# Turning the third and fourth chunks of a layer norm through DRAM and VectorE

## The chip, the cores and the metric

The kernel runs on one core of one Trainium2 chip. The metric is the time of one execution in microseconds (us) of device time. Engines carry the names of the profile: PE (TensorE, matmuls; PEld its weight loads), DVE (VectorE), ACT (ScalarE), POOL (GpSimd) and SP (SyncE, which issues every transfer of this kernel).

## The reference

One transformer block on `x` of 2048 tokens by 512 values: a linear attention and a gated product, each behind a layer norm that six vectors modulate, computed from a condition `c`.

```python
def _A_ref(x, wqkv, wo):                      # 32 heads of 16
    q, k, v = ...                             # x @ wqkv
    phi = lambda t: jnp.where(t > 0, t + 1, jnp.exp(t)) + 1e-6
    pq, pk = phi(q), phi(k)
    kv = jnp.einsum("bhsd,bhse->bhde", pk, v)
    z = jnp.einsum("bhsd->bhd", pk)
    o = jnp.einsum("bhqd,bhde->bhqe", pq, kv) / (jnp.einsum("bhqd,bhd->bhq", pq, z)[..., None] + 1e-6)
    return ... @ wo

def _B_ref(x, w_gate, w_up, w_down):
    return ((x @ w_gate) * (x @ w_up)) @ w_down

sa, ca, ga, sb, cb, gb = ...                  # silu(c) @ w_mod
h = _layernorm(x) * (1 + ca) + sa
x = x + ga * _A_ref(h, A_wqkv, A_wo)
h = _layernorm(x) * (1 + cb) + sb
x = x + gb * _B_ref(h, B_w_gate, B_w_up, B_w_down)
```

## The kernel before

The 2048 tokens are four chunks of four tiles; a tile is 128 tokens by 512 values, tile `i` belongs to chunk `i // 4`. Every fp32 operand of a matmul is split into a high and a low part (`split`: ScalarE copies the high part, VectorE subtracts for the low one), and a product is three matmuls: high by high, high by low, low by high. A projection (`proj`) is 12 matmuls into one PSUM bank.

The order on each engine is the order in which the code is written out; no scheduler moves anything. An engine works through its own queue in that order and waits at an instruction whose operands are not there. SP's queue of transfers is such a queue too.

The changed code is the loop over `i` from 0 to 15 (lines 525 to 587), which makes the keys. In turn `i` it projects the keys of tile `i + 2` (`ahead`), makes their feature map (`k_phi`: two ScalarE passes, `phi_a`, and one VectorE pass, `phi_b`), splits the normalized tile and the keys of tile `i + 1` (`k_split_x` gives `xh` and `xl`, `k_split` gives `kh` and `kl`), adds the keys into `z` (`z_add`) and multiplies the keys of tile `i` with its normalized values (`t_tile`, 12 matmuls into the four accumulators `tacc`). The table `q_at` puts projections of query tiles in between, `extra` the splits of the weights `wv` and `wo` and the sums of the other modulation vectors (`mod_part`).

A projection needs the normalized chunk turned, so that the 512 values lie on the partitions. `Norm` does it in steps: `stats` (VectorE), `rstd_of` (VectorE, then a power on GpSimd), `nmr_of` (VectorE), `xhat` (ScalarE, one pass for each tile), `transpose` (TensorE, four transposes of 128 by 128 into one bank for each of four blocks `k`) and `modulated` (ScalarE scales and shifts the bank into `f`, VectorE casts the high part and subtracts the low one). For chunk 1, 2 and 3 the transposes stand in the loop, eight in each of two turns (`turn_at`): turns 1 and 2 for chunk 1, 4 and 5 for chunk 2, 8 and 9 for chunk 3. The first projection that needs chunk 2 is that of key tile 8, in turn 6; for chunk 3 it is key tile 12, in turn 10.

Behind the loop the row sum of `z` (`row_sum`, split just before) gives `zb`; from it and the accumulators come four tiles `n`, which are split and multiplied with `wv` (`kvps`, 128 by 128 matmuls). The rest of the kernel (from line 636) uses `wo`, turns queries (partly through DRAM: `move_out`, `move_in`, `turn_v`), and runs the second layer norm and the gated product. There, for the last two chunks, the way that the change uses is in place already: tiles go to DRAM, come back with their 32 by 32 blocks moved, VectorE turns each block in place into `wide` (`flip`), and ScalarE takes a row of blocks out of it, scaled and shifted (`flipped`).

Tiles of SBUF come from one pool of 94 buffers (`B`), banks of PSUM from two pools of four.

Of the kernel before, what the change touches and what calls it, by code (L numbers as in the profile page):

```python
# [24 lines left out]
def tile_adaln_block(  # L25
# [42 lines left out]
    def f32(ap):  # L68
        return ap.bitcast(F32)
# [7 lines left out]
    def B(tag, shape=(P, D), dt=F32):  # L77

        return T(tiles, tag, shape, dt)
# [4 lines left out]
    def bank():  # L84
        return T(ps_w, "bank")
# [20 lines left out]
    wide = consts.tile([P, NJ, D], F32, name="wide")  # L106
# [86 lines left out]
    def split(src, h, l, low=None):  # L193
        nc.scalar.activation(h, src, AF.Copy)  # L194
        (low or nc.vector).tensor_tensor(l, src, f32(h), op=ALU.subtract)  # L195
# [23 lines left out]
    def by_row(x):  # L219
        return x.rearrange("p (q s i) -> p s q i", q=NQ, i=BL)  # L220
# [96 lines left out]
                self.t[k] = (h, l)  # L317


    NT = NCH * NJ  # L320
    norm = [Norm(xts[0])]
    wk, wq, wv = [], [], []
    kx, phk, phq, q_ps = {}, {}, {}, {}

    def proj(i, w, of=bank):

        ch, j = divmod(i, NJ)
        ps = of()
# [14 lines left out]
    def k_split_x(i):  # L343
        ch, j = divmod(i, NJ)
        kx[i] = [B("xh", dt=F32R), B("xl", dt=F32R)]
        split(norm[ch].n[j], *kx[i])

    def k_phi(i, ps):
        phi = B("phi")
# [11 lines left out]
    def k_split(i):  # L361
        h, l = B("kh", dt=F32R), B("kl", dt=F32R)
        phi = phk[i]
        nc.scalar.activation(h, phi, AF.Identity, bias=eps_phi)
# [17 lines left out]
    def q_b(i):  # L382
        phi_b(q_ps.pop(i), phq[i])
# [28 lines left out]
    ca = col_out(1, ps_ca, 1.0)  # L412
# [3 lines left out]
    sa = consts.tile([P, KD], F32, name="col0")  # L416
# [47 lines left out]
    nx = Norm(xts[1])  # L464
# [36 lines left out]
    def mod_load(*vs):  # L501
        raw_m.update({v: load_mod(v) for v in vs})

    def mod_part(v, *ks):
        if 0 in ks:
            accs[v] = B("f")
        mod_acc(accs[v], raw_m[v], ks)
# [9 lines left out]
             12: lambda: (mod_part(4, 2, 3), wo_s.extend(split_raw(x) for x in raw_o[:2]), cols.update({3: col_out(3, mod_col(accs[3], bank()), 0.0)}), mod_load(5)),  # L517
             13: lambda: (mod_part(5, 0, 1, 2), wo_s.extend(split_raw(x) for x in raw_o[2:]), cols.update({4: col_out(4, mod_col(accs[4], bank()), 1.0)})),
             14: lambda: (mod_part(5, 3),)}
    pairs = {}  # L520
    q_at = {3: 0, 4: 1, 6: 2, 7: 3}
    ahead = {2: k_ps[2], 3: k_ps[3]}
    turn_at = {4 * ch + j: (ch + 1, 2 * j, 2 * j + 1) for ch in range(1, NCH - 1) for j in range(2)}
    turn_at.update({1: (1, 0, 1), 2: (1, 2, 3)})
    for i in range(NT):
        ch, j = divmod(i, NJ)
        done = 0
        if i > 2:
            ahead[i + 2] = proj(i + 2, wk) if i + 2 < NT else proj(i + 6 - NT, wq)
        if i in q_at:  # L530
# [7 lines left out]
        fresh = i > 0 and ch + 1 < NCH and j == 0  # L538
        if i == 2:
            turn_x()  # L540
            wq.extend(split_blocks(r) for r in raw_q)
        if fresh:
            nx.xhat(2)
        if 0 < i < NT - 1:
            k_split_x(i + 1)
        if fresh:
            nx.xhat(3)
        if 0 < i < NT - 1:
            k_split(i + 1)
        if i in turn_at and i != 2:  # L550
            t_tile(i, 0, 1)
            done = 2
            turn_x()
        if i == 2:
            t_tile(i, *range(KD))
            done = KD
            ahead[i + 2] = proj(i + 2, wk)
        if ch + 2 < NCH and j == 2:
            nx2 = Norm(xts[ch + 2])
            nx2.stats(0, 1)  # L560
        if ch + 2 < NCH and j == 3:
            nx = nx2
            nx.stats(2, 3)
            nx.rstd_of()
            nx.nmr_of()
            nx.xhat(0, 1)
        if i + 2 < NT:
            k_phi(i + 2, ahead.pop(i + 2))
        else:
            q_a(i + 6 - NT, ahead.pop(i + 2))  # L570
            q_b(i + 6 - NT)
        if i in q_at:
            q_a(q_at[i], qps)
            q_b(q_at[i])
        if i + 1 < NT:
            z_add(i + 1)
        if i == NT - 2:
            pairs["z"] = split_raw(zacc, low=nc.gpsimd)
        if i == NT - 1:
            zps = row_sum(pairs["z"])  # L580
            zb = consts.tile([P, D], F32, name="zb")
            nc.scalar.activation(zb, zps, AF.Identity, bias=eps_z)
            zq = B("z")
            nc.gpsimd.tensor_copy(zq.rearrange("p (q s i) -> p q s i", q=NQ, i=BL), by_block(zb))
        t_tile(i, *range(done, KD))
        if i in extra:
            extra[i]()
    ga, sb, cb = rows[2], cols[3], cols[4]
# [130 lines left out]
    def move_out(*tiles):  # L719

        for i in tiles:
            moved[i] = tc.dram_tile([P, D], F32, name=f"moved_{i}")
            nc.sync.dma_start(moved[i], phq.pop(i))

    def move_in(*tiles):

        for i in tiles:
            v = moved[i].rearrange("(m i) (q c) -> q i m c", i=BL, c=P)
            moved[i] = B("u")
            for q in range(NQ):  # L730
                nc.sync.dma_start(moved[i][q * BL:(q + 1) * BL].rearrange("i (m c) -> i m c", c=P), v[q])

    def turn_v(i):

# [163 lines left out]

    def flip(ch, *js):
        for j in js:  # L900
            nc.vector.transpose(wide[:, j].rearrange("p (m s i) -> p m s i", m=NQ, i=BL),
                                blocks.pop((ch, j)).rearrange("p (m s i) -> p m s i", m=NQ, i=BL))

    def flipped(ch, *ks):
        for k in ks:
            f = B("f")
            nc.scalar.activation(f.rearrange("p (x i) -> p x i", i=BL),
                                 wide.rearrange("p j (m s i) -> p (j m) s i", m=NQ, i=BL)[:, :, k],
                                 AF.Identity, scale=cb[:, k:k + 1], bias=sb[:, k:k + 1])
            blocks[ch, "f", k] = f  # L910

    stowed, blocks = {}, {}

# [403 lines left out]
    first[0].sum("s1", "s3", on=nc.gpsimd)  # L1317
    g(lambda: turn_v(13))
    y_seed(13, y_bank)
    norm2[2].xhat_blocks(2, 3)  # L1320
    turn_h(13)
    turn_l(13)
    move_in(14, 15)
    stow(2, 0, 1, 2, 3)
# [107 lines left out]
```

## Time and profile before

| | |
|---|---|
| time, median of 3 runs | 554.86 us (554.34 to 554.95) |
| the profiled execution's own time | 554.37 us |
| its span, from the first to the last instruction | 552.7 us |
| PE busy | 547.0 us (99%), 2488 matmuls |
| DVE, ACT, POOL busy | 373.6 us (68%), 291.7 us (53%), 203.4 us (37%) |
| transfers | 58.28 MB, mean 105 GB/s |
| granted TensorE clock | 1.000 |

A row of a group reads: line, engine, operation, result `<-` operands, count, then busy time and the mean time of one in ns. A row of the timeline reads: start and length in us, engine, line, operation, and in brackets how long the engine had waited and for whom. A row of one line's instructions gives the shortest, the median and the longest in ns. A row of windows gives, for a stretch of time, the sum of busy time, then each engine's busy time and instructions, the granted clock, and the transfer engines' share and rate. The matmuls overlap, so a matmul's length is longer than what it adds to the queue. Names are those of the program, with buffer numbers left out.

### The profile page before, as it was taken

How to read it: one execution, taken by the hardware profiler on the slowest of the kernel's cores; microseconds unless marked ns; L12 is line 12 of the kernel's file. 1: busy time of each engine (PE TensorE's matmuls, PEld its weight loads, DVE VectorE, ACT ScalarE, POOL GpSimd, SP SyncE). 2: the span in 40 equal slices, each digit the busy share in tenths (PEclk: the TensorE clock that was granted, in tenths of full speed). 3: DMA queues.
4: the chain of work that ended last, by engine and by line, in shares of the span. 5: the costliest groups of instructions: out<-in, count | busy, mean ns of one | idle time of the engine just before them, and what ended most of it. 6: DMA issues, size and time to landing. Idle time of an engine off the chain costs nothing.

```text
span 552.7 us, 7324 instructions
## 1 busy us (share of the span) xinstructions
PE 547.0 (99%) x2488; PEld 449.2 (81%) x2488; DVE 373.6 (68%) x610; ACT 291.7 (53%) x539; POOL 203.4 (37%) x204
## 2 busy tenths in 40 slices
PE   8999999999999999999999999999999999999997
PEld 7788888888888878878888888877888888888886
DVE  7896968986887886778776576985444444434434
ACT  3695856646476667566684545454443444444110
POOL 2000000102003201057596666766666546446200
PEclk9999999999999999999999999999999999999999
DMA  8900203320503205845545071690434222200004
GB/s 284 387 15 2 76 20 103 108 77 1 157 2 133 96 5 186 267 145 135 160 111 155 0 230 38 216 322 2 133 116 132 59 57 59 58 20 0 1 0 152
DMA packets 58373, 58.28 MB, mean 105 GB/s; under 512 B 7328, under 2 KB 38304, under 8 KB 58336
## 3 DMA queue, kind: packets, MB, share of 16 engines
q1 hardware_dynamic: 58336, 57.83, 33.2%
q8 instruction: 19, 0.31, 0.2%
q14 instruction: 18, 0.15, 0.1%
HBM read 42.60 MB, written 15.20 MB: 105 GB/s over the span
## 4 chain that ended last, share of the span: by engine, by line
PE 99%; DVE 0%; issue 0%
PE bank L1030 33%; PE acc L766 7%; PE acc L1110 6%; PE acc L1111 6%; PE acc L1112 6%; PE bank L207 5%; PE bank L209 5%; PE bank L208 5%; PE acc L375 3%; PE acc L374 3%; PE acc L373 3%; PE bank L849 2%; PE bank L851 2%; PE bank L850 2%; PE acc L146 2%; PE bank L293 2%
## 5 line engine op out<-in xcount | busy, mean ns | idle before, releaser
L1030 PE MATMUL bank<-h,w 128*128 128x512 f32 (+1 forms) x798 | 184.7, 390 | 0.0
L1030 PEld LDWEIGHTS bank<-h,w 128*128 128x128 f32 (+1 forms) x798 | 148.4, 186 | 33.4 <-ACT bank L1035 0.7
L1035 ACT ACTIVATE bank<-bank 128x512 f32<-128x512 f32 (+1 forms) x38 | 22.2, 583 | 139.6 <-PE bank L1030 139.5
L836 DVE TENSOR_TENSOR x<-acc,x 128x512 f32<-128x512 f32 (+1 forms) x73 | 48.8, 682 | 48.4 <-PE acc L1112 47.7
L1016 POOL TENSOR_TENSOR w<-raw,w 128x256 fp32r<-128x256 f32 (+3 forms) x38 | 40.9, 1077 | 91.0 <-ACT w L1009 91.0
L1111 PE MATMUL acc<-w,kh 128*128 128x512 f32 (+2 forms) x154 | 59.6, 387 | 0.0
L1110 PE MATMUL acc<-w,kh 128*128 128x512 f32 (+2 forms) x154 | 59.6, 387 | 0.0
L1112 PE MATMUL acc<-w,kl 128*128 128x512 f32 (+2 forms) x154 | 59.5, 386 | 0.0
L263 POOL TENSOR_TENSOR rstd<-ve,half 128x4 f32<-128x4 f32 (+1 forms) x10 | 11.0, 1103 | 121.8 <-DVE ve L262 69.6
L195 POOL TENSOR_TENSOR w<-raw,w 128x512 fp32r<-128x512 f32 (+1 forms) x25 | 35.1, 1409 | 52.2 <-ACT w L194 47.3
L1016 POOL TENSOR_TENSOR w<-t,w 128x512 fp32r<-128x512 f32 (+1 forms) x38 | 49.2, 1318 | 0.0
L195 DVE TENSOR_TENSOR kl<-u,kh 128x512 fp32r<-128x512 f32 (+1 forms) x38 | 26.4, 736 | 30.6 <-ACT kh L194 30.6
L207 PE MATMUL bank<-w,h 128*128 128x512 f32 x104 | 40.9, 394 | 0.0
L209 PE MATMUL bank<-w,h 128*128 128x512 f32 x104 | 40.6, 391 | 0.0
L208 PE MATMUL bank<-w,h 128*128 128x512 f32 x104 | 40.6, 390 | 0.0
L766 PE MATMUL acc<-w,xh 128*128 128x512 f32 x120 | 37.4, 393 | 0.0
L1089 DVE TENSOR_TENSOR u<-bank,u 128x512 f32<-128x512 f32 (+1 forms) x19 | 13.1, 691 | 31.6 <-PE bank L1030 25.1
L1110 PEld LDWEIGHTS acc<-w,kh 128*128 128x128 f32 (+1 forms) x154 | 28.9, 188 | 6.0
L1112 PEld LDWEIGHTS acc<-w,kl 128*128 128x128 f32 (+1 forms) x154 | 28.9, 188 | 5.9
L1111 PEld LDWEIGHTS acc<-w,kh 128*128 128x128 f32 (+1 forms) x154 | 28.9, 188 | 5.9
L998 POOL TENSOR_TENSOR t<-raw,t 128x256 f32<-128x256 f32 (+1 forms) x34 | 25.9, 761 | 1.4
L766 PEld LDWEIGHTS acc<-w,xh 128*128 128x128 f32 x120 | 22.2, 188 | 4.6
(211 smaller groups left out, 1116.5 us busy)
## 6 DMA issues: line engine op xcount, KB each, us to landing
raw<-in_w_mod_dram SPq DMA_DIRECT2D x24, 256.0 KB, 3.7
raw<-in_B_w_down_dram SPq DMA_DIRECT2D x20, 256.0 KB, 3.2
raw<-in_B_w_gate_dram SPq DMA_DIRECT2D x36, 128.0 KB, 3.4
raw<-in_B_w_up_dram SPq DMA_DIRECT2D x36, 128.0 KB, 3.4
x<-in_A_x_dram SPq DMA_DIRECT2D x16, 256.0 KB, 5.4
out_dram<-x SPq DMA_DIRECT2D x15, 256.0 KB, 2.6
raw<-in_A_wqkv_dram SPq DMA_DIRECT2D x12, 256.0 KB, 5.4
moved<-h SPq DMA_DIRECT2D x12, 256.0 KB, 2.1
```

Source lines behind the costliest of these rows:

```text
L195: (low or nc.vector).tensor_tensor(l, src, f32(h), op=ALU.subtract)
L207: nc.tensor.matmul(ps, ah, bh, start=i == 0, stop=False)
L208: nc.tensor.matmul(ps, ah, bl, start=False, stop=False)
L209: nc.tensor.matmul(ps, al, bh, start=False, stop=i == n - 1)
L766: nc.tensor.matmul(yps[i], x, y, start=False, stop=k == KD - 1 and x is al, skip_group_check=True)
L836: nc.vector.tensor_tensor(xt[:, a:b], dn[j][:, a:b], xt[:, a:b], op=ALU.add)
L998: sub = lambda out, x, y: (on or nc.gpsimd).tensor_tensor(out, x, y, op=ALU.subtract)
L1016: sub = lambda out, x, y: (on or nc.gpsimd).tensor_tensor(out, x, f32(y), op=ALU.subtract)
L1030: mm = lambda x, y, **kw: nc.tensor.matmul(ps, x[:, k], y, skip_group_check=True, **kw)
L1110: nc.tensor.matmul(ps, hh[:, a:b], dh[:n, c:d], start=i == 0, stop=False)
L1111: nc.tensor.matmul(ps, hh[:, a:b], dl[:n, c:d], start=False, stop=False)
L1112: nc.tensor.matmul(ps, hl[:, a:b], dh[:n, c:d], start=False, stop=i == len(hs) - 1)
```

## The change

Chunks 2 and 3 (`LIFTED`) are no longer transposed by TensorE. Their normalized tiles are written blockwise by ScalarE (`xhat_blocks`), go to DRAM (`lift_out`), come back in four reads each (`lift_in`), are turned by VectorE into `wide` (`lift_turn`), and four rows are taken out by ScalarE (`lift_row`) and split (`lift_parts`: the high part on ScalarE for even rows, on VectorE for odd ones). `k_split_x` reads these chunks' tiles in the blocks' order. Chunk 2's statistics are taken for two tiles at a time, in turns 2 and 3; chunk 3's all in turn 6. The rows of chunk 2 are made in turn 5, those of chunk 3 in turn 9. In turns 6 and 10 the query projection stands in front of the key projection; query tile 4 is projected in turn 10, not in turn 14. The splits of `wo` move from turns 12 and 13 to turns 14 and 15. Some helpers that stood twice in the code are now shared, and one ScalarE pass late in the kernel (`turn_h(13)`) comes in front of two others.

```diff
+    LIFTED = (2, 3)
+    def lift_out(name, x):
+        to = tc.dram_tile([P, D], F32, name=name)
+        nc.sync.dma_start(to, x)
+        return to
+    def lift_in(of):
+        v = of.rearrange("(m i) (q c) -> q i m c", i=BL, c=P)
+        u = B("u")
+        for q in range(NQ):
+            nc.sync.dma_start(u[q * BL:(q + 1) * BL].rearrange("i (m c) -> i m c", c=P), v[q])
+        return u
+    def lift_turn(j, u):
+        nc.vector.transpose(wide[:, j].rearrange("p (m s i) -> p m s i", m=NQ, i=BL),
+                            u.rearrange("p (m s i) -> p m s i", m=NQ, i=BL))
+    def lift_row(k, scale, shift):
+        f = B("f")
+        nc.scalar.activation(f.rearrange("p (x i) -> p x i", i=BL),
+                             wide.rearrange("p j (m s i) -> p (j m) s i", m=NQ, i=BL)[:, :, k],
+                             AF.Identity, scale=scale[:, k:k + 1], bias=shift[:, k:k + 1])
+        return f
+    def lift_parts(k, f, cast=True):
+        h, l = B("h", dt=F32R), B("h", dt=F32R)
+        if k % 2 and cast:
+            nc.vector.tensor_copy(h, f)
+        else:
+            nc.scalar.activation(h, f, AF.Copy)
+        nc.vector.tensor_tensor(l, f, f32(h), op=ALU.subtract)
+        return h, l
...
-        split(norm[ch].n[j], *kx[i])
+        if ch not in LIFTED:
+            split(norm[ch].n[j], *kx[i])
+            return
+        x = by_row(norm[ch].n[j])
+        h, l = (t.rearrange("p (s q i) -> p s q i", q=NQ, i=BL) for t in kx[i])
+        nc.scalar.activation(h, x, AF.Copy)
+        nc.vector.tensor_tensor(l, x, f32(h), op=ALU.subtract)
...
-             12: lambda: (mod_part(4, 2, 3), wo_s.extend(split_raw(x) for x in raw_o[:2]), ...
-             13: lambda: (mod_part(5, 0, 1, 2), wo_s.extend(split_raw(x) for x in raw_o[2:]), ...
-             14: lambda: (mod_part(5, 3),)}
+             12: lambda: (mod_part(4, 2, 3), ...
+             13: lambda: (mod_part(5, 0, 1, 2), ...
+             14: lambda: (mod_part(5, 3), wo_s.extend(split_raw(x) for x in raw_o[:2])),
+             15: lambda: wo_s.extend(split_raw(x) for x in raw_o[2:])}
-    q_at = {3: 0, 4: 1, 6: 2, 7: 3}
+    q_at = {3: 0, 4: 1, 6: 2, 7: 3, 10: 4}
-    turn_at = {4 * ch + j: (ch + 1, 2 * j, 2 * j + 1) for ch in range(1, NCH - 1) for j in range(2)}
-    turn_at.update({1: (1, 0, 1), 2: (1, 2, 3)})
+    turn_at = {1: (1, 0, 1), 2: (1, 2, 3)}
     for i in range(NT):
         ch, j = divmod(i, NJ)
-        if i > 2:
+        up = ch + 1 if 0 < ch < NCH - 1 else None
+        if i in (6, 10):
+            qps = proj(q_at[i], wq)
+        if i > 2 and i != NT - 2:
             ahead[i + 2] = proj(i + 2, wk) if i + 2 < NT else proj(i + 6 - NT, wq)
-        if i in q_at:
+        if i in q_at and i not in (6, 10):
             qps = proj(q_at[i], wq)
...
-        if fresh:
-            nx.xhat(2)
+        if ch + 2 < NCH and j == 3:
+            nx = nx2
+            if ch == 0:
+                nx.nmr_of(0, 2)
+            nx.xhat_blocks(0, 1)
+            lifts = [lift_out(f"first_{ch}_{n}", nx.n[n]) for n in range(2)]
+            if ch:
+                nx.nmr_of(2, 4)
+                nx.xhat_blocks(2, 3)
+                lifts += [lift_out(f"first_{ch}_{n}", nx.n[n]) for n in (2, 3)]
+                lifts = [lift_in(x) for x in lifts]
         if 0 < i < NT - 1:
             k_split_x(i + 1)
-        if fresh:
-            nx.xhat(3)
-        if 0 < i < NT - 1:
             k_split(i + 1)
+        if up and j == 1:
+            if up == 2:
+                lift_turn(2, lifts[2])
+                lift_turn(3, lifts[3])
+            for k in range(KD):
+                nx.t[k] = lift_parts(k, lift_row(k, ca, sa))
+            norm[up:] = [nx]
...
             nx2.stats(0, 1)
-        if ch + 2 < NCH and j == 3:
-            nx = nx2
+            nx2.rstd_of(0, 2)
+            if ch:
+                nx2.stats(2, 3)
+                nx2.nmr_of(0, 2)
+                nx2.rstd_of(2, 4)
+        if ch == 0 and j == 3:
             nx.stats(2, 3)
-            nx.rstd_of()
-            nx.nmr_of()
-            nx.xhat(0, 1)
+            nx.rstd_of(2, 4)
...
+        if ch == 0 and j == 3:
+            nx.nmr_of(2, 4)
+            nx.xhat_blocks(2, 3)
+            lifts[0], lifts[1] = lift_in(lifts[0]), lift_in(lifts[1])
+            lifts += [lift_out(f"first_{ch}_{n}", nx.n[n]) for n in (2, 3)]
+            lifts[2], lifts[3] = lift_in(lifts[2]), lift_in(lifts[3])
...
         t_tile(i, *range(done, KD))
+        if up == 2 and j == 0 or ch == 1 and j == 3:
+            lift_turn(0, lifts[0])
+            lift_turn(1, lifts[1])
+        if up == 3 and j == 0:
+            lift_turn(2, lifts[2])
+            lift_turn(3, lifts[3])
```

More of the change, by code (lines that the diff above doesn't have):

```diff
@@ L516, in tile_adaln_block @@
              11: lambda: (mod_part(3, 3), mod_part(4, 0, 1), rows.update({2: mod_row(2, pairs[2])}), raw_o.extend(load(wo_v[k], "raw") for k in range(2, KD))),
-             12: lambda: (mod_part(4, 2, 3), wo_s.extend(split_raw(x) for x in raw_o[:2]), cols.update({3: col_out(3, mod_col(accs[3], bank()), 0.0)}), mod_load(5)),
-             13: lambda: (mod_part(5, 0, 1, 2), wo_s.extend(split_raw(x) for x in raw_o[2:]), cols.update({4: col_out(4, mod_col(accs[4], bank()), 1.0)})),
-             14: lambda: (mod_part(5, 3),)}
+             12: lambda: (mod_part(4, 2, 3), cols.update({3: col_out(3, mod_col(accs[3], bank()), 0.0)}), mod_load(5)),
+             13: lambda: (mod_part(5, 0, 1, 2), cols.update({4: col_out(4, mod_col(accs[4], bank()), 1.0)})),
+             14: lambda: (mod_part(5, 3), wo_s.extend(split_raw(x) for x in raw_o[:2])),
+             15: lambda: wo_s.extend(split_raw(x) for x in raw_o[2:])}
     pairs = {}
-    q_at = {3: 0, 4: 1, 6: 2, 7: 3}
+    q_at = {3: 0, 4: 1, 6: 2, 7: 3, 10: 4}
     ahead = {2: k_ps[2], 3: k_ps[3]}
-    turn_at = {4 * ch + j: (ch + 1, 2 * j, 2 * j + 1) for ch in range(1, NCH - 1) for j in range(2)}
-    turn_at.update({1: (1, 0, 1), 2: (1, 2, 3)})
+    turn_at = {1: (1, 0, 1), 2: (1, 2, 3)}
     for i in range(NT):
@@ L536, in turn_x @@
             norm[to:] = [nx]
-        fresh = i > 0 and ch + 1 < NCH and j == 0
         if i == 2:
@@ L560, in tile_adaln_block @@
             nx2.stats(0, 1)
-        if ch + 2 < NCH and j == 3:
-            nx = nx2
+            nx2.rstd_of(0, 2)
[4 more added lines that the diff above has]
+        if ch == 0 and j == 3:
             nx.stats(2, 3)
-            nx.rstd_of()
-            nx.nmr_of()
-            nx.xhat(0, 1)
+            nx.rstd_of(2, 4)
         if i + 2 < NT:
             k_phi(i + 2, ahead.pop(i + 2))
-        else:
+        elif i == NT - 1:
             q_a(i + 6 - NT, ahead.pop(i + 2))
@@ L721, in move_out @@
         for i in tiles:
-            moved[i] = tc.dram_tile([P, D], F32, name=f"moved_{i}")
-            nc.sync.dma_start(moved[i], phq.pop(i))
+            moved[i] = lift_out(f"moved_{i}", phq.pop(i))
     def move_in(*tiles):
         for i in tiles:
[L728 to L731, printed above, removed]
+            moved[i] = lift_in(moved[i])
     def turn_v(i):
@@ L900, in flip @@
         for j in js:
-            nc.vector.transpose(wide[:, j].rearrange("p (m s i) -> p m s i", m=NQ, i=BL),
-                                blocks.pop((ch, j)).rearrange("p (m s i) -> p m s i", m=NQ, i=BL))
+            lift_turn(j, blocks.pop((ch, j)))
     def flipped(ch, *ks):
         for k in ks:
[L906 to L910, printed above, removed]
+            blocks[ch, "f", k] = lift_row(k, cb, sb)
     stowed, blocks = {}, {}
@@ L1319, in tile_adaln_block @@
     y_seed(13, y_bank)
+    turn_h(13)
     norm2[2].xhat_blocks(2, 3)
-    turn_h(13)
     turn_l(13)
```

## The prediction

> **What bounds the kernel now.** I read the page first: engines, slices, chain.
>
> ```profile
> span 552.7 us, 7324 instructions
> PE 547.0 (99%) x2488; PEld 449.2 (81%) x2488; DVE 373.6 (68%) x610; ACT 291.7 (53%) x539; POOL 203.4 (37%) x204
> PE   8999999999999999999999999999999999999997
> DVE  7896968986887886778776576985444444434434
> PE 99%; DVE 0%; issue 0%
> ```
>
> TensorE is busy in every slice and is 99% of the chain that ended last, so an instruction taken from its queue is time won, unless TensorE must then wait. The changed code lies in the third to tenth slices (28 to 138 us), where VectorE (DVE) is at 6 to 9 tenths: it has little room, and it gets more work. The question is whether each new operand is there when TensorE comes for it.
>
> I make the sum against the profiled execution, 554.37 us (span 552.7), and move the difference to the median of three runs, 554.86, which lies 0.5 above it. Runs spread over 0.6, so about 0.2%, 1.1 us, is what a measurement can tell from no change.
>
> **What TensorE is rid of.** Two windows of the trace, one around the products of tile 2 (no turning) and one around those of tile 4, which has eight transposes in its middle; the first number is TensorE's busy time.
>
> ```profile
> 46.10:48.89 2.79, 2.79 (x14) 2.25 (x12) 2.54 (x7) 0.00 (x0) 0.00 (x0) 1.00 0.01 3
> 54.40:58.05 3.65, 3.65 (x21) 3.08 (x20) 2.99 (x6) 3.65 (x7) 0.00 (x0) 1.00 0.00 0
> L293 PE MATMUL bank<-ident,n x80: 270/272/274, 32.0 to 219.5; 128*128 128x128 f32 x80
> ```
>
> Both stages run at full clock (1.00) and differ by eight transposes: 3.65 - 2.79 = 0.86 us. The third and fourth chunks have 16 transposes each, so 32 go: 4 x 0.86 = 3.44 us. The projections that move are neither more nor fewer.
>
> The rows of single transposes say 272 ns, and 32 of them would be 8.7 us; but matmuls overlap, and the windows decide. The Trainium skill, TensorE: Matmul & The Clock Gate, Part 4 (PE-mode transpose), gives about 275 ns for one in a kernel's context: 8.8 us for 32, an estimate from that page. The trace agrees with the duration and not with that saving.
>
> **What takes their place.** Per chunk: four normalized tiles go out to DRAM and come back by 16 reads, all from SyncE's queue; VectorE turns four tiles; ScalarE scales four rows out of `wide`. The casts of half the rows go from VectorE to ScalarE. These operations run elsewhere in the trace:
>
> ```profile
> L901 DVE STREAM_TRANSPOSE wide<-u x8: 671/703/714, 287.8 to 331.6; 128x512 f32<-128x512 f32 x8
> L907 ACT ACTIVATE f<-wide,col,col x8: 800/805/817, 302.8 to 345.7; 128x512 f32<-128x512 f32 x8
> L225 ACT ACTIVATE w<-raw x4: 630/632/633, 36.5 to 38.1; 128x512 fp32r<-128x512 f32 x4
> L226 DVE TENSOR_TENSOR w<-raw,w x4: 684/684/684, 39.2 to 41.0; 128x512 fp32r<-128x512 f32 x4
> moved<-h SPq DMA_DIRECT2D x12, 256.0 KB, 2.1
> u<-moved SPq DMA_DIRECT2D x48, 64.0 KB, 2.0
> 242.71 5.86 SPq L731 DMA_DIRECT2D u<-moved  x12
> ```
>
> Four VectorE passes of 0.684 start between 39.2 and 41.0, one each 0.60; ScalarE's copies each 0.53; a turn takes 0.70, next start 0.62 (an estimate by the same overlap). Blockwise reading costs nothing extra (L225 and L226 read blockwise), so the new form of `k_split_x` is free. SyncE needs 5.86/12 = 0.49 per read, landing takes 2.0 to 2.1. Per chunk VectorE gets 4 x 0.62 and sheds 2 x 0.46, net 1.6 us more.
>
> **Third chunk, step by step.** Up to the statistics at 42.85 every queue holds what it held, so I start there.
>
> ```profile
> 41.97 0.62 ACT L194 ACTIVATE xh<-n 128x512 fp32r<-128x512 f32 x1
> 42.85 0.68 DVE L242 BATCH_NORM_STATS2 st<-x 128x6 f32<-128x512 f32 x1
> 44.36 0.18 DVE L243 BATCH_NORM_AGGREGATE mv<-st 128x2 f32<-128x6 f32 x1
> 44.46 0.66 DVE L341 SCALAR_TENSOR_TENSOR phi<-bank,phi 128x512 f32<-128x512 f32 x1
> 48.35 0.18 DVE L243 BATCH_NORM_AGGREGATE mv<-st 128x2 f32<-128x6 f32 x1
> 48.57 0.17 DVE L262 TENSOR_SCALAR ve<-mv 128x4 f32<-128x4 f32 x1
> 50.15 1.52 ACT L272 ACTIVATE n<-x,nmr,rstd 128x512 f32<-128x512 f32 x2 [4.27 <-DVE nmr L267]
> 51.58 0.58 ACT L337 ACTIVATE phi<-bank 128x512 f32<-128x512 f32 x1
> 52.72 0.58 ACT L337 ACTIVATE h<-bank 128x512 f32<-128x512 f32 x1
> 52.85 0.69 DVE L341 SCALAR_TENSOR_TENSOR phi<-bank,phi 128x512 f32<-128x512 f32 x1 [2.74 <-ACT phi L338]
> 55.81 0.71 ACT L364 ACTIVATE kh<-phi,eps_phi 128x512 fp32r<-128x512 f32 x1
> 56.43 1.45 ACT L305 ACTIVATE f<-bank,col,col 128x512 f32<-128x512 f32 x2
> 57.24 0.43 DVE L313 CAST h<-f 128x512 fp32r<-128x512 f32 x1
> 57.70 0.69 DVE L316 TENSOR_TENSOR h<-f,h 128x512 fp32r<-128x512 f32 x1
> 64.39 0.39 PE L207 MATMUL bank<-w,h 128*128 128x512 f32 x1
> ```
>
> The steps they give: statistics of two tiles 1.61 (42.85 to 44.46); last aggregate to `ve` 0.22; `ve` to the first normalized tile 1.58 (48.57 to 50.15, through GpSimd's power); normalizing 0.715 each; a pair of exponentials 1.14, and 1.27 from its start to VectorE's use; `kh` 0.62; a cast 0.46.
>
> - `ve` 44.36 + 0.22 = 44.58, tile 0 of the chunk on ScalarE at 46.16, tile 1 at 46.87.
> - Now queued behind these two: `xh` of key tile 4, at 47.58 where it stood at 41.97. VectorE waits for it until 48.24, `kl` 48.86, then the other statistics 49.46 to 51.07, `ve` 51.19, tiles 2 and 3 at 52.77 and 53.48.
> - ScalarE then runs without a gap: `xh` 54.20, `kh` 54.73, exponentials 55.35 and 56.49. VectorE gets the second pair's result at 57.76, then one step each 0.60: `z` 58.36, turns 58.96 and 59.58, a `wv` low part 60.20, `xl` 60.80, `kl` 61.40, turns 62.00 and 62.62, the last done 63.32.
> - Transfers: tile 2 goes out at 53.6, has landed at 55.7; eight reads at 0.49 until 59.6, the last landed 61.1. Its turn stands at 62.62: hidden, with 1.5 us to spare. Without that cover each us late is one us of stall. Tiles 0 and 1 are back by about 55, four before their turns.
> - Rows: `f` 63.35, `h` 64.15, low part 64.81; row 1 `f` 64.68, cast 65.52, low part 65.98; row 2 `f` 65.39, `h` 66.20, low part 66.86; row 3 `f` 66.73, cast 67.57, low part 68.03, done 68.72.
>
> TensorE began projection 8 at 64.39. Without 16 transposes (1.72) and with a query projection (2.79) in front it begins at 65.46, when row 0 is ready (64.78). Twelve matmuls of 0.233 put the last at 68.02, and it needs 68.72: 0.7 late, with the stops of the earlier rows about **0.9 us of stall**. Some 35 steps carry perhaps 0.02 each: bounds 0.2 and 1.6. So the third chunk wins 1.72 and gives half of it back.
>
> **Fourth chunk.** All its statistics run together, and its turns have a whole tile more. From low part 3 of one chunk to that of the next VectorE holds 25 passes of 0.60, two casts, four statistics of 0.81 and four turns (15.0 + 0.9 + 3.2 + 2.5), and I estimate 1.7 for two modulation sums and the small ones, 23.3 us: from 68.6 to 91.9 if it never waits. TensorE reaches the last matmul of projection 12 after projections 9, 3, 10, 11, 4 and four groups of key products: 69 + 9 x 2.79 + 2.5, about 96.6. Of these 4.7 us VectorE loses 2.9 where tile 8's split stands behind four normalizings (4 x 0.715), and I estimate about 1 at exponentials: little is left. I take **0.2 us**, bounds 0 and 0.8, the upper one since 16 reads of 0.49 are 7.8 us and the fourth tile lands close before its turn.
>
> **The end of the loop.** Query tile 4 now comes at tile 10, and tile 14 has no projection; `wo`'s splits stand at tiles 14 and 15.
>
> ```profile
> 118.79 1.29 DVE L195 TENSOR_TENSOR w<-raw,w 128x512 fp32r<-128x512 f32 x2
> 122.01 0.69 DVE L341 SCALAR_TENSOR_TENSOR h<-bank,h 128x512 f32<-128x512 f32 x1 [0.66 <-ACT h L338]
> 125.95 0.62 PE L183 MATMUL bank<-w,ones_r 128*128 128x512 f32 x2
> 127.32 0.67 ACT L582 ACTIVATE zb<-bank,eps_z 128x512 f32<-128x512 f32 x1
> 127.45 0.69 DVE L341 SCALAR_TENSOR_TENSOR h<-bank,h 128x512 f32<-128x512 f32 x1 [3.49 <-ACT h L338]
> 128.05 0.68 DVE L599 TENSOR_REDUCE den<-zb 128x32 f32<-128x512 f32 x1
> 131.73 2.49 DVE L195 TENSOR_TENSOR w<-n,w 128x512 fp32r<-128x512 f32 x4
> 135.66 0.27 PE L208 MATMUL bank<-w,w 128*128 128x128 f32 x1
> ```
>
> The row sum comes 2.79 sooner after tile 13, but `z` too is about 2.5 sooner, as neither a query tile (0.66 of waiting and one step) nor two `wo` low parts (1.2) stand before it: I cost it at nothing, at most 0.3. Behind the row sum, VectorE's reduction now follows two low parts that wait for ScalarE's copies behind `zb`: first copy 127.89 to 128.52, low parts 128.55 and 129.15, reduction 129.75 instead of 128.05. The last low part of `n` was done at 134.22 and is used at 135.66: 1.44 of cover against 1.7 of delay, **0.2 us**, bounds 0 and 0.7. The `xhat_blocks` line late in the kernel is ScalarE order beside idle time: nothing.
>
> Sum: 3.44 - 0.9 - 0.2 - 0.2 = 2.1 won: span 550.6, profiled time 552.2, median **552.7**.
>
> **The rivals.**
> - *Nothing waits*: the steps above overlap more tightly and every operand is in time: 3.4 won, 551.4. For it: the stall is the end of a long sum. Against: from 57.76 to the last turn VectorE works in it without a gap. 0.15.
> - *The queues are later*: stalls at their upper bounds, 1.6 + 0.8 + 0.7 = 3.1: 0.3 won, 554.5, not told from no change. 0.18.
> - *The round trip is late*, and the time ends slower: the in-order SyncE queue holds reads until the write has landed, and VectorE's turn holds all behind it. Where the transfer engines are loaded, landing is slow:
>
> ```profile
> h<-side_s SPq DMA_DIRECT2D x6, 256.0 KB, 5.7
> ```
>
> With 5.7 for write and read, tile 3 lands at 53.6 + 5.7 + 3.9 - 0.5 + 5.7 = 68.4, 5.8 after its turn's place: stall 6.7, net 3.3 lost, 558.1. It costs from 1.5 us of lateness, and ends slower than before from about 3.6 (1.1 more to be measurable). Against: the window of tile 4 shows the transfer engines at 0.00. 0.10. The Trainium skill, VectorE: DVE Perf Modes, The three transpose paths, warns that a plain DMA that transposes by strides is 19 times slower than the crossbar path when the innermost destination stride is large; here the read keeps runs of 128 values and only moves blocks, and the trace agrees with no such penalty (2.0 us).
> - *Transposes cost their full 272 ns*: 8.7 - 1.3 won, 547.5. The windows speak against it. 0.02.
>
> The forecast itself has 0.55. Faster by over 0.2% are it, nothing waits, and the full price: 0.72. Same 0.18, slower 0.10. The range runs from 551.3 (nothing waits) to 555.0 (over the late queues); outside are the late round trip, the full price and the edges, under 2 in 10.
>
> **What would show it.** Right: L293 has 48 transposes; between 65 and 69 us TensorE's first waits, at projection 8, on ScalarE's or VectorE's `h`, in sum about 0.9; the four turns of a chunk with no wait on `u`; waits of a few tenths near 96 and 132; nothing new behind 140. Wrong: VectorE waiting for `u` at a turn (late round trip), waits over 2 us at projection 8 or 12 (late queues), or none at all; and a span that shrinks by other than 3.44 less the new waits means that the price of a transpose is wrong.

## The result and the profile after

The changed kernel takes 552.21 us in the median of 6 runs (551.79 to 552.59); the kernel before, beside it, 554.77. The ratio is 0.9951, 95% interval 0.9939 to 0.9962: 2.6 us faster. The forecast was 552.7, faster.

The page of the changed kernel: span and engines, two rows of the slices, and the engines of the chain that ended last.

```profile
span 550.1 us, 7373 instructions
PE 544.3 (99%) x2456; PEld 445.7 (81%) x2456; DVE 378.8 (69%) x618; ACT 294.2 (53%) x543; POOL 203.5 (37%) x206
PE   8999999999999999999999999999999999999997
DVE  7897779989987876869766576985444344434444
PE 97%; DVE 1%; ACT 0%; issue 0%; DVEq 0%
```

TensorE has 32 instructions fewer and 2.7 us less work (547.0 before), and still fills every slice. New is that 2% of the chain that ended last now runs through other engines: somewhere TensorE waits. Its waits between 40 and 165 us (engine, tile and line, whom it waited for: us in all, times, longest) are these; the kernel before has none there.

```profile
PEld bank L209 <- DVE h L352: 1.0, 3, 0.4
PEld bank L207 <- DVE h L349: 0.3, 1, 0.3
PEld bank L208 <- DVE w L195: 0.2, 1, 0.2
```

The first two are projection 8 with the third chunk's rows; the last stands at the key-value products, at 132.95 us. Waits of the weight loads partly overlap running matmuls, so for what a wait costs I take the times at which TensorE reaches the same work. The first row of each pair is the first matmul of the three projections in front of tile 3, the second a group of query turns well behind the changed code; before, then after.

```profile
37.89 0.39 PE L207 MATMUL bank<-w,h 128*128 128x512 f32 x1
160.93 0.60 PE L701 MATMUL bank<-ident,h 128*128 128x128 f32 x4
```

```profile
37.67 0.39 PE L207 MATMUL bank<-w,h 128*128 128x512 f32 x1
158.28 0.60 PE L771 MATMUL bank<-ident,h 128*128 128x128 f32 x4
```

From the one to the other it is 123.04 us before and 120.61 after: 2.43 won. I call this the stretch. The first 38 us are code that nobody changed, and they vary between executions (the first row stood between 37.56 and 39.53 in eleven of the twelve profiles below), so that 0.22 of the 2.65 between the second rows is not the change's. The spans of the two profiled executions differ by 2.6, so nothing of size comes or goes behind the second row; the moved ScalarE pass late in the kernel is worth next to nothing.

Inside the stretch the changed kernel wins 1.01 up to projection 10 (the third chunk's 16 transposes are worth 1.72, and 0.71 is lost at projection 8); another 1.79 up to the row sum of `z`; and it loses 0.37 behind that, 0.36 of it by the row sum of the modulation vector `gb`: 1.01 + 1.79 - 0.37 = 2.43. The row sum of `z` stands at 125.95 before (shown in the prediction). Here are that of `gb` before, then both after:

```profile
139.90 0.68 PE L183 MATMUL bank<-w,ones_r 128*128 128x512 f32 x2
```

```profile
122.93 0.62 PE L183 MATMUL bank<-w,ones_r 128*128 128x512 f32 x2
137.24 0.68 PE L183 MATMUL bank<-w,ones_r 128*128 128x512 f32 x2
```

From the one to the other it is 13.95 before and 14.31 after.

How projection 8 waits, in the rows of ScalarE and VectorE of the changed kernel, and the first `t_tile` matmul behind it:

```profile
62.83 0.82 ACT L341 ACTIVATE f<-wide,col,col 128x512 f32<-128x512 f32 x1 [3.91 <-DVE wide L336]
63.68 0.63 ACT L351 ACTIVATE h<-f 128x512 fp32r<-128x512 f32 x1
65.51 0.69 DVE L352 TENSOR_TENSOR h<-f,h 128x512 fp32r<-128x512 f32 x1
67.59 0.69 DVE L352 TENSOR_TENSOR h<-f,h 128x512 fp32r<-128x512 f32 x1
65.19 0.39 PE L207 MATMUL bank<-w,h 128*128 128x512 f32 x1
68.67 0.40 PE L414 MATMUL acc<-kh,xh 128*128 128x512 f32 x1
```

Row 0 is there (64.31) when TensorE comes at 65.19, but the low parts come one after another, the last at 68.28, and the twelve matmuls that would take 2.77 take 3.48.

### The profile page after: what moved, and what is told of

Read it like the earlier page. It is cut to its first block, busy times and chain, and to the rows that moved or that the text cites. A ratio compares the mean times of both kernels' runs of the same rounds, so it can differ in the third digit from the quotient of the medians.

```text
span 550.1 us, 7373 instructions
## 1 busy us (share of the span) xinstructions
PE 544.3 (99%) x2456; PEld 445.7 (81%) x2456; DVE 378.8 (69%) x618; ACT 294.2 (53%) x543; POOL 203.5 (37%) x206
## 4 chain that ended last, share of the span: by engine, by line
PE 97%; DVE 1%; ACT 0%; issue 0%; DVEq 0%
PE bank L1091 33%; PE acc L832 7%; PE acc L1171 6%; PE acc L1173 6%; PE acc L1172 6%; PE bank L209 5%; PE bank L207 4%; PE bank L208 4%; PE acc L416 3%; PE acc L414 3%; PE acc L415 2%; PE bank L917 2%; PE bank L915 2%; PE bank L916 2%; PE acc L146 2%; PE acc L942 1%
## 5 line engine op out<-in xcount | busy, mean ns | idle before, releaser
L263 POOL TENSOR_TENSOR rstd<-ve,half 128x2 f32<-128x2 f32 (+1 forms) x12 | 11.7, 978 | 119.3 <-DVE ve L262 66.8
L207 PE MATMUL bank<-w,h 128*128 128x512 f32 x104 | 40.9, 394 | 0.0
L209 PE MATMUL bank<-w,h 128*128 128x512 f32 x104 | 40.9, 393 | 0.0
```

Source lines behind the costliest of these rows:

```text
L207: nc.tensor.matmul(ps, ah, bh, start=i == 0, stop=False)
L209: nc.tensor.matmul(ps, al, bh, start=False, stop=i == n - 1)
```

## The experiments

All twelve, each with the median, that of the kernel before in the same set of runs, and the change of the stretch against 123.04. Unless said otherwise the diff is against the changed kernel.

| run | median | before | difference | stretch |
|---|---|---|---|---|
| third_only | 556.63 | 554.99 | +1.64 | +1.47 |
| third_stats | 554.13 | 554.72 | -0.59 | -0.57 |
| fourth_only | 553.92 | 554.99 | -1.07 | -1.41 |
| keys_first | 556.39 | 554.72 | +1.67 | +1.11 |
| early_stats | 551.57 | 554.99 | -3.42 | -3.18 |
| wo_pool | 552.64 | 554.99 | -2.35 | -2.10 |
| wo_back | 552.56 | 554.72 | -2.16 | -2.09 |
| late12 | 556.73 | 554.72 | +2.01 | +1.32 |
| late4 | 552.31 | 554.52 | -2.21 | -2.03 |
| dummy | 554.29 | 554.52 | -0.23 | -0.63 |
| stats_wo14 | 551.22 | 554.52 | -3.30 | -3.58 |
| after_again | 552.52 | 554.52 | -2.00 | -2.40 |

The two columns agree within some 0.7 us; where less matters I go by the stretch. The last row is the changed kernel once more, so that the three runs above it have it beside them:

> The changed kernel itself, on the chip of this set of runs, to be set beside the other three: 552.2 us.

**One chunk alone.** First the third chunk, with the fourth turned by TensorE as before.

```diff
-    LIFTED = (2, 3)
+    LIFTED = (2,)
-    turn_at = {1: (1, 0, 1), 2: (1, 2, 3)}
+    turn_at = {1: (1, 0, 1), 2: (1, 2, 3), 8: (3, 0, 1), 9: (3, 2, 3)}
... statistics and xhat of chunk 3 where the kernel before has them (turns 6, 7 and 8)
```

> Only the third chunk is turned by VectorE; the fourth chunk's 16 transposes are on TensorE again. Everything else is the changed kernel. Theory (the prediction's): 1.72 us of transposes go, about 0.7 comes back as waits at projection 8, and about 0.36 stays lost at the end of the loop (wo's splits), so 0.65 less than before: 554.1 us, with the waits at projection 8 still there. Rival (the loss at projection 8 is made by the two lifted chunks together, since the fourth chunk's early statistics share VectorE with the third's rows): no wait at projection 8, 553.4 us.

It is slower than the kernel before by 1.64 us, ratio 1.0034 (1.0022 to 1.0046). Both forecasts miss. Up to projection 10 it wins the same 1.01 as the changed kernel, and the waits at projection 8 are the same two rows (L209 and L207), so the rival falls: they are the third chunk's own. But a wait appears that neither foresaw:

```profile
PEld bank L293 <- ACT n L272: 2.1, 2, 1.1
```

TensorE stands 2.1 us at the fourth chunk's transposes. Whom ScalarE waits for there, first in the kernel before, then in this run (the second pair's statistics on VectorE, and the normalizing on ScalarE):

```profile
74.41 0.69 DVE L242 BATCH_NORM_STATS2 st<-x 128x6 f32<-128x512 f32 x1
77.73 1.52 ACT L272 ACTIVATE n<-x,nmr,rstd 128x512 f32<-128x512 f32 x2 [4.71 <-DVE nmr L267]
```

```profile
77.78 0.69 DVE L242 BATCH_NORM_STATS2 st<-x 128x6 f32<-128x512 f32 x1
81.10 1.52 ACT L272 ACTIVATE n<-x,nmr,rstd 128x512 f32<-128x512 f32 x2 [5.48 <-DVE nmr L267]
```

Counted from the stretch's start (37.89 before, 38.93 here) the same step comes 2.33 us later, and TensorE 1.01 sooner. VectorE makes the third chunk's four rows in one go up to 69.56 here, 30.6 after the start; the kernel before had made them in two pairs by 65.80, 27.9 after it. Everything queued behind slides. 1.72 - 0.71 - 2.1 - 0.37 (the end of the loop) = -1.46; the stretch says -1.47. The changed kernel has no such wait. It takes the fourth chunk's four statistics in one go, a turn earlier. The next run adds that alone:

```diff
+            if ch:
+                nx2.stats(2, 3)
+                nx2.nmr_of(0, 2)
+                nx2.rstd_of(2, 4)
... (to third_only, in turn 6; the statistics of turn 7 go)
```

> As the run with only the third chunk turned by VectorE (556.6 us), but the fourth chunk's four statistics are taken in one go at tile 6, as the changed kernel has them; its 16 transposes stay on TensorE. Theory: that run lost 2.1 us of TensorE's time at the fourth chunk's transposes because the second pair of statistics stood one tile later in a VectorE queue that the third chunk's turning had pushed back by 3.4 us; taken in one go the normalized tiles are there in time, the 2.1 go: about 554.5 us, and no wait at the fourth chunk's transposes. Rival (VectorE is simply too full, wherever the statistics stand): the same work, the same lateness, 556.6 us.

554.13, and no wait at L293 is left: the theory, by 0.4 better than its 554.5 (its 3.4 us are raw times, 1.04 of which is that run's later start). The second pair's statistics now start at 74.99 and the normalizing at 78.16 with no idle time in front of it, 38.6 after the start of the stretch (39.53) where third_only had 42.2:

```profile
74.99 0.69 DVE L242 BATCH_NORM_STATS2 st<-x 128x6 f32<-128x512 f32 x1
78.16 1.50 ACT L272 ACTIVATE n<-x,nmr,rstd 128x512 f32<-128x512 f32 x2
```

VectorE's statistics are the same four; where they stand in its queue decides.

The fourth chunk alone (`LIFTED = (3,)`, the third as in the kernel before, its query projection behind the keys):

> Only the fourth chunk is turned by VectorE; the third chunk is turned by TensorE as before, with its query projection behind the key projection again. Theory: 1.72 us of transposes go with no wait at projection 12, 0.36 is lost at the end of the loop: 1.36 less than before, 553.4 us. Rival (each chunk gives half its gain back in some form): about 0.9 less at most, 553.9 us, with waits between 85 and 100 us.

553.92, which as a time is the rival's (553.9), not the theory's 553.4. Against the kernel before in its own set it is 1.07 less, between the two. The rival's sign, waits between 85 and 100 us, is absent: of the three waits only that at the key-value products is left, so 1.72 won, 0.36 lost, 1.36 by the sum and 1.41 by the stretch. The two chunks alone give +1.47 and -1.41, with the loss at the end of the loop in each; together they give -2.43. They are not additive: what makes the third chunk's turning pay is a piece of the fourth's.

**The query projection in front.**

```diff
-        if i in (6, 10):
-            qps = proj(q_at[i], wq)
-        if i in q_at and i not in (6, 10):
+        if i in q_at:
             qps = proj(q_at[i], wq)
```

> The changed kernel with the key projection in front of the query projection again at tiles 6 and 10. Theory: TensorE comes to projection 8 2.79 us sooner while its last operand stays at about 68.3, so the waits there grow from 0.7 to 3.5; at projection 12 the last low part (94.9) then also comes after TensorE, 0 to 1.9 more: 555.0 to 556.9 us, slower than before. Rival (the order is without weight, because VectorE's queue, shorter by the later query tile, brings the rows sooner): 552.2 us.

556.39, slower than before, as the theory has it. Projection 8 now begins with a long wait:

```profile
65.28 0.50 PE L207 MATMUL bank<-w,h 128*128 128x512 f32 x1 [1.80 <-ACT h L351]
```

TensorE comes out of turn 6's projections 2.79 us later than in the changed kernel (33.79 against 31.00 after the stretch's start): to the hundredth the query projection that no longer covers the rows. At projection 12 another 0.71 is lost. Without this swap, at the two tiles, the whole change would have been slower than the kernel before.

**The third chunk's statistics in one go.**

```diff
             nx2.stats(0, 1)
             nx2.rstd_of(0, 2)
-            if ch:
-                nx2.stats(2, 3)
-                nx2.nmr_of(0, 2)
-                nx2.rstd_of(2, 4)
+            nx2.stats(2, 3)
+            nx2.nmr_of(0, 2)
+            nx2.rstd_of(2, 4)
... all four tiles normalized, sent out and read back at the head of turn 3
```

> The changed kernel with the third chunk's statistics all four in one go one tile earlier, as the fourth chunk has them, and its four tiles normalized and sent out together. Theory: the end of the third chunk's chain is VectorE's work between the second pair's statistics and the rows; taking two statistics (1.5 us) out of it frees projection 8 and the 0.7 of waits goes: 551.5 us. Rival (ScalarE's queue sets the chain): four normalizings (2.9 us) now stand ahead of tile 4's split, VectorE idles there instead, the rows come no earlier and the time stays 552.2 us.

551.57: the theory. Rows come 1.27 us earlier, and projection 8 runs through (the first row is ScalarE's first of the four, the second VectorE's last low part, then TensorE):

```profile
61.56 0.82 ACT L341 ACTIVATE f<-wide,col,col 128x512 f32<-128x512 f32 x1 [3.91 <-DVE wide L336]
66.32 0.69 DVE L352 TENSOR_TENSOR h<-f,h 128x512 fp32r<-128x512 f32 x1
65.19 0.39 PE L207 MATMUL bank<-w,h 128*128 128x512 f32 x1
67.96 0.39 PE L414 MATMUL acc<-kh,xh 128*128 128x512 f32 x1
```

From the first matmul to the next group it is 2.77 instead of 3.48: all 0.71 is back, and 0.04 more by the stretch. The run moves more than two statistics: their two normalizings on ScalarE move with them. In the changed kernel these stand in front of tile 5's split, and VectorE waits for it:

```profile
54.39 0.69 DVE L195 TENSOR_TENSOR xl<-n,xh 128x512 fp32r<-128x512 f32 x1 [1.51 <-ACT xh L194]
```

In this run that wait is gone. So it shows that the second pair's place is the cause; how much of the 1.27 is VectorE's queue and how much ScalarE's it does not part.

**The end of the loop.** Three places for the low parts of `wo`. On GpSimd:

```diff
-             14: lambda: (mod_part(5, 3), wo_s.extend(split_raw(x) for x in raw_o[:2])),
-             15: lambda: wo_s.extend(split_raw(x) for x in raw_o[2:])}
+             14: lambda: (mod_part(5, 3), wo_s.extend(split_raw(x, low=nc.gpsimd) for x in raw_o[:2])),
+             15: lambda: wo_s.extend(split_raw(x, low=nc.gpsimd) for x in raw_o[2:])}
```

> The changed kernel with the four low parts of wo's splits on GpSimd, so that VectorE has none of them at the end of the loop. Theory: the 0.36 us lost between the row sum of z and the key-value products comes from those low parts in front of VectorE's reduction; it goes: 551.85 us. Rival (the loss is ScalarE's copies of wo behind zb, or GpSimd is slower at them and holds z back): no change or slower, 552.2 to 552.8 us.

552.64; the stretch is 0.33 longer than the changed kernel's, where the theory had it 0.36 shorter. The time is the rival's; its reasons are not what the trace shows. Counted from the stretch's start (38.00 here) the reduction behind `zb` comes 1.72 sooner (at 125.35; 126.74 in the changed kernel), so the low parts did stand in its way, and the row sum of `z` isn't held back (85.24 after the start; 85.26). But the two small steps behind it, 0.18 each in the changed kernel, are long:

```profile
126.05 1.19 DVE L670 TENSOR_SCALAR den<-den 128x32 f32<-128x32 f32 x1
127.28 1.22 DVE L671 COPY den0q<-den 128x32 f32<-128x32 f32 x1
125.91 2.54 POOL L195 TENSOR_TENSOR w<-raw,w 128x512 fp32r<-128x512 f32 x2
```

```profile
127.45 0.18 DVE L670 TENSOR_SCALAR den<-den 128x32 f32<-128x32 f32 x1
127.66 0.18 DVE L671 COPY den0q<-den 128x32 f32<-128x32 f32 x1
```

Two GpSimd subtractions of 1.27 run from 125.91 to 128.45, and each of the small steps ends as one of them ends (127.24 and 128.50). They cost 2.05 more: 2.05 - 1.72 = 0.33. The Trainium skill, SBUF — State Buffer, Who interferes with whom, has the rule: VectorE and GpSimd share a pair of ports, which a copy or a `tensor_scalar` of VectorE can need, and the loser waits for the whole of the other's instruction. The trace agrees.

At tiles 12 and 13, as before:

```diff
-             12: lambda: (mod_part(4, 2, 3), cols...
+             12: lambda: (mod_part(4, 2, 3), wo_s.extend(split_raw(x) for x in raw_o[:2]), cols...
... the other two in turn 13, none in turns 14 and 15
```

> The changed kernel with wo's splits (ScalarE copies and VectorE low parts) back at tiles 12 and 13, where the kernel before has them. Theory: two low parts in front of VectorE's reduction lengthen the stretch from the row sum of z to the key-value products' end by 0.36 us; without them it is 13.95 again as before instead of 14.31: 551.85 us. Rival (VectorE just fits around tiles 12 to 14): the low parts push z's sum back there, the row sum of z waits, and the time is 552.2 us or more.

552.56, stretch 0.34 longer than the changed kernel's: the time is the rival's, and each mechanism is there in its place. Behind the row sum of `z` the loss is gone (from the next `t_tile` to the row sum of `gb` 13.47; 13.85 in the changed kernel, 13.49 before). But the row sum itself now waits:

```profile
PEld bank L183 <- POOL w L195: 0.9, 1, 0.9
```

Two low parts (1.2 us) stand in front of the last addition into `z`. So the move of `wo`'s splits in the change was needed; it bought the row sum of `z` for 0.36.

**The round trip.** More reads on SyncE's queue, of data that nobody uses:

```diff
+            for _ in range(3):
+                lift_in(again)
             lifts[2], lifts[3] = lift_in(lifts[2]), lift_in(lifts[3])
```

> The changed kernel with 12 more reads of 64 KB (unused copies of the chunk's first tile) on SyncE's queue ahead of the reads of the third chunk's tiles 2 and 3: 12 x 0.47 = 5.6 us later. Theory (the prediction's late round trip: cover of 1.0 to 1.5 us, then each us late is one us of stall): tile 3 lands at about 66.7 instead of 61.1, its turn waits 4.6 us, and the time is 552.2 + 4.6 = 556.8 us, slower than before. Rival (the reads overlap on the transfer engines, or VectorE catches up behind the turn): under 1 us, 552.2 to 553.2 us.

556.73, slower than before; the stretch is 3.75 longer than the changed kernel's. Now VectorE waits for `u`, twice, and behind it TensorE (3.1 at projection 8). SyncE's queue and VectorE's turns in this run, and SyncE's in the changed kernel:

```profile
54.23 9.68 SPq L332 DMA_DIRECT2D u<-first  x20
63.33 0.71 DVE L336 STREAM_TRANSPOSE wide<-u 128x512 f32<-128x512 f32 x1 [1.82 <-DMA u<-first]
65.60 0.71 DVE L336 STREAM_TRANSPOSE wide<-u 128x512 f32<-128x512 f32 x1 [1.56 <-DMA u<-first]
```

```profile
55.27 3.64 SPq L332 DMA_DIRECT2D u<-first  x8
```

The last read is issued at 63.91 instead of 58.91, 5.0 later and not 5.6, since the first two unused reads fill a time in which SyncE waited for the written tile. The last turn stands at 65.60 instead of 62.13: 3.5 late, so 1.5 of the 5.0 were covered. The forecast had 4.6; the mechanism stands. This profiled execution is the fastest of its twelve: by the medians, each against the kernel before in its set, the loss is 4.0 to 4.6.

With 4 reads in place of 12:

> As the run with 12 unused reads, with 4: they fill the 1.0 us that SyncE waits for the written tile anyway, then push the reads of tiles 2 and 3 back by 4 x 0.48 - 1.0 = 0.9 us. Theory (tile 3 lands about 1.5 us before its turn): the lateness is covered, no wait on u at the turns, 552.2 us. Rival (no cover: what is added to the queue is added to the stall): 0.9 to 1.9 us more, 553.1 to 554.1 us.

552.31 beside 552.52 of the changed kernel: nothing. No turn of the third chunk waits for `u`, and TensorE leaves turn 6's projections 31.08 after the stretch's start (31.00). The stretch of this profiled execution is 0.40 longer all the same. Its delay begins at the fourth chunk, with 0.37 on VectorE: VectorE's second turn there waits for its transfer, first in the changed kernel, then in this run.

```profile
84.97 0.71 DVE L336 STREAM_TRANSPOSE wide<-u 128x512 f32<-128x512 f32 x1 [0.57 <-DMA u<-first]
```

```profile
88.78 0.71 DVE L336 STREAM_TRANSPOSE wide<-u 128x512 f32<-128x512 f32 x1 [0.92 <-DMA u<-first]
```

Everything on VectorE behind it comes 0.37 later after the stretch's start, up to the last low part, and TensorE, with a cover of 0.2 in the changed kernel (below), waits at projection 12. The wait at this turn was 0.34 to 0.67 in nine profiles with the fourth chunk turned by VectorE, 0.92 here and 1.04 in keys_first, where projection 12 waits too. Whether the unused reads, which lie some 20 us earlier, have a part in it isn't shown. (The granted clock was lower ahead of the stretch, 0.72 from 12 to 24 us, and 1.00 from 24 to 36.)

**The price of a transpose.**

```diff
+        if i in (8, 9):
+            t_tile(i, 0, 1)
+            done = 2
+            for _ in range(2):
+                ps = bank()
+                for b in range(NJ):
+                    nc.tensor.transpose(ps[:, b * P:(b + 1) * P], ident, ident)
```

> The changed kernel with 16 transposes of a constant added on TensorE, in the places at tiles 8 and 9 where the kernel before turned the fourth chunk; nobody reads the result. Theory (the windows' price, 0.86 us for eight): 1.72 us more, 553.9 us. Rival (each costs its 272 ns): 4.35 us more, 556.6 us.

554.29 beside 552.52: 1.77 more, and 1.77 by the stretch (against the changed kernel of the same set). Windows around the projection in front of tile 8 and around tile 8's products with the first eight:

```profile
79.92:82.64 2.72, 2.72 (x13) 2.25 (x12) 1.90 (x3) 2.66 (x6) 0.00 (x0) 1.00 0.66 216
82.64:86.26 3.62, 3.62 (x22) 3.08 (x20) 2.97 (x5) 3.34 (x7) 0.00 (x0) 1.00 0.52 138
```

0.90 for eight, 0.11 for one: the price of the windows. The 272 ns of a single row are its length in the pipeline.

**Both losses taken away.** `early_stats`, and the four splits of `wo` all in turn 14:

```diff
+             14: lambda: (mod_part(5, 3), wo_s.extend(split_raw(x) for x in raw_o))}
```

> The third chunk's statistics in one go (551.6 us when run alone), and wo's four splits all at tile 14. There VectorE idles from about 120.7 to 124.4 us in the changed kernel, so the four low parts cost nothing, and none stands in front of the reduction behind zb. Theory: the stretch from the row sum of z to the end of the key-value products is 0.36 us shorter, as in the kernel before: 551.2 us, with no wait of TensorE between 40 and 160 us. Rival (four copies on ScalarE behind z's copy delay the query tile's exponentials and zb by 0.2 to 0.5, which eats the gain): 551.6 us.

551.22 (550.56 to 552.25) beside 552.52 of the changed kernel and 554.52 of the one before: ratio to the latter 0.9941 (0.9929 to 0.9953), the lowest time of all. The medians don't part it from early_stats (3.30 and 3.42 below the kernel before in their sets); the stretch does, 3.58 and 3.18. VectorE's rows show where the four fit, in what was idle time up to the query's feature map:

```profile
120.87 3.17 DVE L195 TENSOR_TENSOR w<-raw,w 128x512 fp32r<-128x512 f32 x4 [0.56 <-ACT w L194]
123.97 0.68 DVE L376 SCALAR_TENSOR_TENSOR h<-bank,h 128x512 f32<-128x512 f32 x1
124.57 0.67 DVE L655 TENSOR_REDUCE den<-zb 128x32 f32<-128x512 f32 x1
```

From the row sum of `z` to that of `gb` it is 13.95, as in the kernel before (14.31 in the changed one). No wait of the changed stages is left on TensorE, and the stretch is 3.58 shorter than before: the 3.44 of the transposes, all of it, with 0.14 unexplained.

## Why the prediction was right

- *32 transposes are worth 3.44 us.* Right: added back 16 cost 1.77, and with nothing waiting 3.58 are won. The rival with 272 ns each falls.
- *Third chunk: 1.72 won, 0.9 lost at projection 8.* Right in place and mechanism, 0.71 measured. The last low part was done at 68.28 (forecast 68.72), TensorE came at 65.19 (65.46). The cause given, the second pair of statistics and all that is queued behind it, is shown by early_stats: with the pair a turn earlier the wait is gone. That it is VectorE's queue alone is not shown, since the pair's normalizings on ScalarE moved with it.
- *The query projection in front.* Counted as 2.79 of cover: keys_first lost exactly that at projection 8.
- *The round trip has 1.5 us to spare, and each us beyond is a us of stall.* Right for the third chunk: 0.9 of delay cost nothing there, 5.0 cost 3.75. The rival of the late round trip is a real mechanism that didn't arise there: no turn waited for `u`. In the fourth chunk one did, by 0.57, against the sign named in the prediction (four turns with no wait). It was the second tile's turn, not the fourth's as the upper bound had it, and it used up cover instead of stopping TensorE.
- *Fourth chunk: 0.2, bounds 0 and 0.8.* It was 0, narrowly, and in part by luck. The last low part is done at 95.63 and the last matmul of projection 12 begins at 95.81, a cover of 0.2, while the wait at the second tile's turn differs by more than that between profiles; in late4 it was 0.35 longer, and TensorE waited.

```profile
94.94 0.69 DVE L352 TENSOR_TENSOR h<-f,h 128x512 fp32r<-128x512 f32 x1
95.81 0.39 PE L209 MATMUL bank<-w,h 128*128 128x512 f32 x1
```

- *End of the loop: row sum 0, products 0.2.* Row sum right; products 0.36. The delay was sized well (row sum to reduction 3.81 instead of 2.10: 1.71, forecast 1.7), the cover was 1.35 instead of 1.44.
- *Sum.* With the measured sizes 3.44 - 0.71 - 0 - 0.36 = 2.37, and 2.43 by the stretch; the forecast was 2.1. The terms were off by 0.19, 0.2 and -0.16, which partly cancel.

What the prediction did not see is that its parts hang on each other. It gave the fourth chunk's statistics in one go no weight beyond "all its statistics run together"; third_only and third_stats show that without it the delay which the third chunk's turning puts on VectorE stops TensorE for 2.1 us at the fourth chunk and makes the kernel slower, at least where TensorE still turns the fourth chunk (both chunks turned by VectorE, with the fourth's statistics in two pairs, was not run). The forecast was of the whole and so came out right, but its row for the third chunk, "wins 1.72 and gives half of it back", isn't what that part does alone.

## What to carry to other kernels

Where one engine is 99% busy, price what leaves its queue by windows with and without it, not by the length of single rows; then ask for every operand that now comes from a longer chain when it is there and what stands behind it on the engine that makes it. An engine with room on average (VectorE at 69%) can still pass a delay on by its order: moving two statistics, one projection or four subtractions within their queues was worth 2.1, 2.79 and 0.4 us here, beside 3.44 for the transposes. Test the parts of a change alone and together; they need not add up.

## What the runs showed of the hardware

- VectorE's small fp32 copy and `tensor_scalar` of 128x32 took 1.22 and 1.19 us instead of 0.18 in wo_pool while GpSimd ran subtractions of 128x512, and ended when those ended. A VectorE pass from a PSUM bank (124.74, `h<-bank,h`) beside another of these subtractions kept its 0.69, and the reduction beside GpSimd's copy kept its 0.67. A VectorE subtraction of 128x512 was stretched in the changed kernel: the first of `wo`'s low parts took 1.37 instead of 0.68 (from 121.67) while GpSimd's subtraction for `z` ran (121.19 to 122.49).
- In late12 the weight loads waited for 3.1 us and no matmul ran from 65.24 to 67.87. The granted clock then was 0.50 from about 67.4 to 70.6 and 1.00 again from 70.8; the rows of two windows of 3 us say 0.73 and 0.70. In keys_first, with a wait of 2.2 us of the weight loads (1.8 without a matmul), it stayed at 1.00 from 60 to 72 us.

```profile
66.00:69.00 3.00, 1.13 (x3) 0.79 (x3) 1.43 (x3) 2.62 (x4) 0.00 (x0) 0.73 0.82 271
67.60:70.60 3.00, 2.73 (x7) 2.05 (x7) 2.49 (x4) 2.97 (x6) 0.00 (x0) 0.50 0.36 133
69.00:72.00 3.00, 3.00 (x11) 2.20 (x9) 2.65 (x5) 2.94 (x6) 0.00 (x0) 0.70 0.02 8
72.00:75.00 3.00, 3.00 (x14) 2.45 (x14) 3.00 (x6) 2.97 (x6) 0.00 (x0) 1.00 0.00 0
```
